# The last few microseconds of an attention and mixer kernel: order of the last chunks, and columns of the last stores

## The chip, the cores and the metric

One core of a Trainium2 chip. The metric is the device time of one execution in microseconds (us). A time is some 2 us longer than the span that the profile shows (the profiled run of the kernel before took 406.0 us and its span is 403.9 us).

## The reference, cut to what matters

```python
# batch 8, 12 heads, 448 rows, head 64; d_model 768, d_tok 256, d_ch 1536
x  = attention(normalised q, normalised k, v)          # 8 x 448 x 768
u  = x + (relu(x.T @ w_tok1) @ w_tok2).T               # mixes the rows
out = u + relu(u @ w_ch1) @ w_ch2                      # mixes the channels
```

Only the last product, `relu(...) @ w_ch2`, the addition of `u` and the store of `out` are touched by the change.

## The kernel before

The 448 rows of a batch are three chunks of 128 rows and 64 rest rows. The rest rows of two batches are done together as one chunk of 128 partitions (`m == NC`), with the odd batch. For each chunk the second channel product is done in two halves of 384 columns, each 12 matmuls into PSUM (the memory that matmuls write), and the addition of `u` on VectorE writes the half into `ost`, a tile in SBUF (the memory that stores are read from here). When both halves are there, the chunk is stored. The chunk of rest rows goes to two places in memory, so it needs two stores of 64 rows.

```python
    def m_ch2(b, m, dh):
        ...
        for ct in range(CT):                                   # CT = 12
            nc.tensor.matmul(psF[:], gt[:, ct, lo:lo + P], wc2t[:, ct, dh * DH:(dh + 1) * DH], ...)
        nc.vector.tensor_tensor(out=o[:, dh * DH:(dh + 1) * DH]..., in0=psF[:]..., in1=urt[b]..., op=ALU.add)
        if dh == NDH - 1:
            if m < NC:
                nc.sync.dma_start(out=out[b, 0:SM].rearrange("(p c) d -> c p d", c=NC)[m], in_=o[:])
            else:
                nc.sync.dma_start(out=out[b - 1, SM:S, :], in_=o[0:XR])      # XR = 64
                nc.sync.dma_start(out=out[b, SM:S, :], in_=o[XR:P])

    def ch_units(b):
        return ([...m_ch1(b, ct)... for ct in range(CT)]
                + [(ns(DH, 12), lambda m=m, dh=dh: m_ch2(b, m, dh))
                   for m in range(NC + b % 2) for dh in range(NDH)])         # rest rows last
```

Of the kernel before, what the change touches and what calls it, by code (L numbers as in the profile page):

```python
# [7 lines left out]
FP32 = mybir.dt.float32  # L8
FP16 = mybir.dt.float16
AF = mybir.ActivationFunctionType  # L10
ALU = mybir.AluOpType
# [11 lines left out]
def kernel(  # L23
# [12 lines left out]
    nc = tc.nc  # L36

    B, H, S, E = q.shape
# [4 lines left out]
    P = 128  # L43
    NC = 3
    SM = P * NC
    XR = S - SM
    E1 = E + 1
    DT = D // P
    CT = C // P
    TT = T // P  # L50
    DH = 384
    NDH = D // DH
# [17 lines left out]
    ps = ctx.enter_context(tc.tile_pool(name="ps", bufs=4, space=bass.MemoryType.PSUM))  # L70
# [8 lines left out]
    wc2t = cst.tile([P, CT, D], FP16, name="wc2t")  # L79
# [12 lines left out]
    pairt, urt = {}, {}  # L92
# [287 lines left out]
    def m_ch1(b, ct):  # L380
        ut, gt = pairt[b // 2]
        sp = slice(S * (b % 2), S * (b % 2 + 1))
        psG = ps.tile([P, S], FP32, name=f"psG_{b}_{ct}", tag="b")
        for dt in range(DT):
            nc.tensor.matmul(psG[:], wc1t[:, dt, ct * P:(ct + 1) * P], ut[:, dt, sp],  # L385
                             start=(dt == 0), stop=(dt == DT - 1))
        nc.scalar.activation(out=gt[:, ct, sp], in_=psG[:], func=AF.Relu)  # L387

    ost = {}

    def m_ch2(b, m, dh):
        gt = pairt[b // 2][1]
        lo = SM if m == NC else (512 * (b % 2) + P * m)
        if dh == 0:
            ost[0] = outp.tile([P, D], FP32, name=f"ost_{b}_{m}", tag="ost")
        o = ost[0]
        psF = ps.tile([P, DH], FP32, name=f"psF_{b}_{m}_{dh}", tag="b")
        for ct in range(CT):
            nc.tensor.matmul(psF[:], gt[:, ct, lo:lo + P], wc2t[:, ct, dh * DH:(dh + 1) * DH],  # L399
                             start=(ct == 0), stop=(ct == CT - 1))  # L400
        j = m if b % 2 == 0 else (m + 1) % 4
        nc.vector.tensor_tensor(out=o[:, dh * DH:(dh + 1) * DH].rearrange("p (i d) -> p i d", i=3),  # L402
                                in0=psF[:].rearrange("p (i d) -> p i d", i=3),
                                in1=urt[b][:, 3 * dh:3 * dh + 3, j, :], op=ALU.add)
        if dh == NDH - 1:
            if m < NC:
                nc.sync.dma_start(out=out[b, 0:SM].rearrange("(p c) d -> c p d", c=NC)[m], in_=o[:])
            else:
                nc.sync.dma_start(out=out[b - 1, SM:S, :], in_=o[0:XR])
                nc.sync.dma_start(out=out[b, SM:S, :], in_=o[XR:P])  # L410



    def ns(cols, n=1):
        return n * cols / 2.4

    def ch_units(b):
        return ([(ns(S, DT), lambda ct=ct: m_ch1(b, ct)) for ct in range(CT)]
                + [(ns(DH, 12), lambda m=m, dh=dh: m_ch2(b, m, dh))
                   for m in range(NC + b % 2) for dh in range(NDH)])  # L420

    queue = []
    fed = [0.0]
# [58 lines left out]
    with tc.manual_schedule():  # L482
# [5 lines left out]
            name=nc.get_next_instruction_name(), act_func_set_id=ACT_SET_LN_EXP,  # L488
# [34 lines left out]
        w = ps.tile([P, 512], FP32, name="busy", tag="b")  # L523
# [36 lines left out]
        for i in range(NP_ALL + 2):  # L560
# [27 lines left out]
            def tok2(p):  # L588
                m_tok2(p)
                if p % NPAIR == NPAIR - 1:  # L590
                    queue.extend(ch_units(p // NPAIR))
# [133 lines left out]
```

## Time and profile before

| | before |
|---|---|
| median of 6 runs, first comparison | 406.39 us (406.03 to 407.37) |
| span of the profiled run | 403.9 us |
| TensorE busy | 96% |
| end of the last matmul | 398.95 us |
| from there to the end of the span ("the tail") | 4.95 us |

In the views PE is TensorE, PEld its weight loads, DVE VectorE, ACT ScalarE, POOL GpSimd; SPq and ACTq are the sync and the scalar queue, from which stores are issued. A store's data move some time after its issue, as packets on 16 DMA engines; it has landed when all of it is reported done.

The head of the page of the kernel before, and its chain of waits (shares of the span):

```profile
span 403.9 us, 9103 instructions
PE 389.7 (96%) x3646; PEld 225.6 (56%) x3646; DVE 204.9 (51%) x463; ACT 226.4 (56%) x407; POOL 208.8 (52%) x306
...
PE 77%; POOL 6%; issue 5%; ACT 5%; DVE 4%; SPq 1%; DMA 1%; POOLq 0%; DVEq 0%
```

TensorE is busy nearly everywhere, so without fewer matmuls time can be won only where it has nothing to do. That is 403.9 - 389.7 = 14.2 us in all: 4.66 us in the first 20 us (the windows view shows it busy for 15.34 of them), 4.6 us scattered, and 4.95 us at the end, with which the change deals. The timeline of the kernel before, from 383 us (TensorE alone) and then from 399 us (all engines); the columns are start, duration, engine, line, operation:

```profile
383.19 15.76 PE L399 MATMUL psF<-wc2t,gt 128*128 128x384 f16 x96
```

```profile
398.99 0.56 DVE L402 TENSOR_TENSOR ost<-psF,ur 128x384 f32<-128x384 f32 x1 [1.39 <-PE psF L399]
399.58 0.50 SPq L409 DMA_DIRECT2D out_dram<-ost  x1
400.13 0.58 SPq L410 DMA_DIRECT2D out_dram<-ost  x1
```

The 96 matmuls of the last batch's four chunks end at 383.19 + 15.76 = 398.95 us. What follows is serial: an addition, two issues, the landing of their data, and the closing semaphores.

In the DMA view (from issue to landing, last number, us) the stores of the last chunk stand against it:

```profile
out_dram<-ost SPq DMA_DIRECT2D x2, 192.0 KB, 2.7
```

```profile
out_dram<-ost SPq DMA_DIRECT2D x1, 384.0 KB, 2.3
```

### The profile page before, as it was taken

The numbers are of one execution on the slowest core, as the hardware profiler recorded it, in microseconds if no ns is written. First come the engines' busy times: TensorE is split into PE (matmuls) and PEld (weight loads), VectorE is DVE, ScalarE is ACT, GpSimd is POOL, SyncE is SP. The second block draws the span as 40 slices with busy tenths as digits, with TensorE's granted clock in tenths as the row PEclk, the third lists the DMA queues.
The fourth block names the chain that finished last, engine by engine and source line by source line (L and its number), as shares of the span: only waits on it lengthen the run. The fifth ranks groups of instructions, "written<-read, shape, count | busy, mean of one in ns | idle before, by whom it ended". The sixth has DMA issues, their size and how long they took to land.

```text
span 403.9 us, 9103 instructions
## 1 busy us (share of the span) xinstructions
PE 389.7 (96%) x3646; PEld 225.6 (56%) x3646; DVE 204.9 (51%) x463; ACT 226.4 (56%) x407; POOL 208.8 (52%) x306
## 2 busy tenths in 40 slices
PE   7799999999999999999999999999999999999995
PEld 3356465565555565555555565555555565565562
DVE  5698689574444655355544654455534342242021
ACT  6998699633766356654756436664766435611400
POOL 5987495795292939385673909476773400000000
PEclk9699999999999999999999999999999999999998
DMA  8999999999792978989893798979882643023012
GB/s 223 283 270 261 219 242 199 225 231 197 184 204 52 250 177 211 182 213 179 232 202 60 227 147 214 212 149 236 185 132 50 141 97 67 15 66 93 2 78 78
DMA packets 137194, 67.51 MB, mean 167 GB/s; under 512 B 93184, under 2 KB 133568, under 8 KB 137152
## 3 DMA queue, kind: packets, MB, share of 16 engines
q1 hardware_dynamic: 132976, 61.36, 70.5%
q0 software_dynamic: 3632, 5.18, 7.2%
q8 instruction: 28, 0.46, 0.5%
q10 hardware_dynamic: 544, 0.39, 0.3%
q14 instruction: 14, 0.11, 0.1%
HBM read 43.38 MB, written 11.01 MB: 135 GB/s over the span
## 4 chain that ended last, share of the span: by engine, by line
PE 77%; POOL 6%; issue 5%; ACT 5%; DVE 4%; SPq 1%; DMA 1%; POOLq 0%; DVEq 0%
PE psF L399 24%; PE psG L385 23%; PE psO L318 7%; PE psS L297 7%; PE psR L338 4%; PE psU L357 4%; PE psX L304 3%; ACT pt L298 2%; PE psO L320 2%; POOL kq L207 2%; POOL sq L176 2%; POOL kq L218 1%; PE pst L239 1%; POOL sqx L176 1%; DVE ssq L189 1%
## 5 line engine op out<-in xcount | busy, mean ns | idle before, releaser
L298 ACT ACTIVATE pt<-psS 128x896 f16<-128x896 f32 x141 | 124.0, 915 | 71.6 <-PE psS L297 71.3
L385 PE MATMUL psG<-ut,wc1t 128*128 128x448 f16 x576 | 122.5, 353 | 0.0
L399 PE MATMUL psF<-wc2t,gt 128*128 128x384 f16 x672 | 117.1, 326 | 0.6 <-ACT pt L305 0.6
L387 ACT ACTIVATE gt<-psG 128x448 f16<-128x448 f32 x96 | 52.3, 545 | 79.2 <-PE psG L385 79.0
L207 POOL TENSOR_TENSOR kq<-km,rn 128x384 f16<-128x384 f32 x47 | 39.7, 844 | 101.9 <-ACT rn L200 93.2
L399 PEld LDWEIGHTS <-gt 128*128 128x128 f16 x672 | 63.4, 98 | 42.6 <-issue 4.7
L385 PEld LDWEIGHTS <-wc1t 128*128 128x128 f16 x576 | 52.5, 98 | 46.2 <-issue 5.2
L402 DVE TENSOR_TENSOR ost<-psF,ur 128x384 f32<-128x384 f32 x56 | 31.2, 557 | 81.0 <-PE psF L399 77.5
L318 PEld LDWEIGHTS <-pt 128*128 128x128 f16 x1152 | 52.3, 98 | 16.7 <-issue 5.6
L318 PE MATMUL psO<-vt,pt 128*128 128x65 f16 x1152 | 57.9, 194 | 0.1
L189 DVE TENSOR_REDUCE ssq<-sq 128x12 f32<-128x768 f32 (+1 forms) x49 | 45.2, 932 | 17.9 <-POOL sq L176 14.4
L297 PE MATMUL psS<-qk 64*128 64x448 f16 x282 | 44.0, 360 | 1.2 <-ACT pt L298 1.2
L324 DVE TENSOR_TENSOR x<-psO,rec 128x256 f16<-128x256 f32 x96 | 40.8, 424 | 3.3
L320 PE MATMUL psO<-vx,pt 128*128 128x130 f16 x192 | 42.0, 219 | 0.0
L207 POOL TENSOR_TENSOR kq<-qm,rn 128x384 f16<-128x384 f32 x47 | 39.0, 830 | 0.0
L323 DVE RECIPROCAL rec<-psO 128x4 f32<-128x4 f32 x96 | 17.1, 178 | 41.0 <-PE psO L320 40.8
L176 POOL TENSOR_TENSOR sq<-km 128x384 f32<-128x384 f32 x42 | 34.5, 824 | 2.5 <-DMA km<-in_k_dram 2.4
L367 DVE TENSOR_TENSOR ut<-psU,xT 128x448 f16<-128x448 f32 (+2 forms) x39 | 17.6, 477 | 26.2 <-PE psU L357 17.8
L338 PE MATMUL psR<-x,w1t 128*128 128x128 f16 x384 | 29.4, 219 | 0.1
L297 PEld LDWEIGHTS <-qk 64*128 64x128 f16 x282 | 10.5, 94 | 30.6 <-issue 27.4
L357 PE MATMUL psU<-w2t,r 128*128 128x448 f16 x96 | 25.9, 353 | 1.6 <-DVE x L324 0.8
L305 ACT ACTIVATE pt<-psX 128x448 f16<-128x448 f32 x48 | 26.1, 544 | 0.0
(75 smaller groups left out, 339.9 us busy)
## 6 DMA issues: line engine op xcount, KB each, us to landing
vm<-in_v_dram SPq DMA_DIRECT2D x16, 576.0 KB, 7.1
out_dram<-ost SPq DMA_DIRECT2D x24, 384.0 KB, 2.9
qm<-in_q_dram SPq DMA_DIRECT2D x15, 576.0 KB, 5.1
km<-in_k_dram SPq DMA_DIRECT2D x15, 576.0 KB, 6.9
wc1t<-in_moe_w_ch_dram POOLq DMA_DIRECT2D x2, 1152.0 KB, 13.3
wc2t<-in_moe_w_ch_dram POOLq DMA_DIRECT2D x2, 1152.0 KB, 13.2
out_dram<-ost SPq DMA_DIRECT2D x8, 192.0 KB, 2.8
xq<-in_q_dram SPq DMA_DIRECT2D x7, 192.0 KB, 7.8
```

The source lines that it names most:

```text
L176: eng.tensor_tensor(out=out, in0=src, in1=src, op=ALU.mult)
L189: nc.vector.tensor_reduce(out=ssqs[p // HP % 3][:, lo + 6 * a0:lo + 6 * a1], in_=sq[p][:, a0:a1].rearrange("p a g e -> p (a g) e"), axis=A ...
L207: eng.tensor_tensor(out=kqs[n % 2][:, j, a, 0:NC, :].rearrange("p c (g e) -> p g c e", g=2), in0=src, in1=_bcast_free(rn, E), op=ALU.mult)
L297: nc.tensor.matmul(psS[:, g, 0:S], qk[r, P * c:P * (c + 1)], qk[r, 512:512 + S], start=True, stop=True)
L298: nc.scalar.activation(out=pt[:, 2 * S * c:2 * S * (c + 1)].rearrange("p (g s) -> p g s", g=2), in_=psS[:, :, 0:S], func=AF.Exp, scale=inv ...
L318: nc.tensor.matmul(psO[:, mm, E1 * g:E1 * (g + 1)], pt[:, at:at + P], vt[:, 2 * j + g, c, 0:E1], start=(g == 0 and c == 0), stop=False)
L320: nc.tensor.matmul(psO[:, mm, :], pt[:, PX + lo:PX + lo + P], vx[:, j, 0:2 * E1], start=False, stop=True)
L338: nc.tensor.matmul(psR[:, tt, :], w1t[:, m, tt * P:(tt + 1) * P], xs[p][:, m, :], start=(m == 0), stop=(m == NC))
L357: nc.tensor.matmul(psU[:], rs[p][:, tt, :], w2t[:, tt, lo:lo + S], start=(tt == 0), stop=by_dma and tt == TT - 1)
L385: nc.tensor.matmul(psG[:], wc1t[:, dt, ct * P:(ct + 1) * P], ut[:, dt, sp], start=(dt == 0), stop=(dt == DT - 1))
L387: nc.scalar.activation(out=gt[:, ct, sp], in_=psG[:], func=AF.Relu)
L399: nc.tensor.matmul(psF[:], gt[:, ct, lo:lo + P], wc2t[:, ct, dh * DH:(dh + 1) * DH], start=(ct == 0), stop=(ct == CT - 1))
```

## The change

Its intent is to shorten the serial tail: the rest rows with their two stores go two chunks earlier, and the last chunk's second half is done as 256 and then 128 columns. Each of its parts is stored by itself, so that only 64 KB are left to store after the last matmul.

```diff
-    def m_ch2(b, m, dh):
+    def m_ch2(b, m, i0, i1, send=False):        # columns 128*i0 to 128*i1
...
-        if dh == NDH - 1:
+        if send or i1 == DT:
+            cols = slice(P * ost[1], P * i1)     # what is not stored yet
+            ost[1] = i1
             if m < NC:
-                nc.sync.dma_start(out=...[m], in_=o[:])
+                nc.sync.dma_start(out=...[m][:, cols], in_=o[:, cols])
             else:
-                nc.sync.dma_start(out=out[b - 1, SM:S, :], in_=o[0:XR])
-                nc.sync.dma_start(out=out[b, SM:S, :], in_=o[XR:P])
+                nc.sync.dma_start(out=out[b - 1, SM:S, cols], in_=o[0:XR, cols])
+                nc.sync.dma_start(out=out[b, SM:S, cols], in_=o[XR:P, cols])
...
+        last = b == B - 1
+        for m in (0, NC, 1, 2) if last else range(NC + b % 2):
+            for i0, i1 in ((0, 3), (3, 5), (5, 6)) if last and m == 2 else ((0, 3), (3, 6)):
+                units.append((ns(P * (i1 - i0), CT), lambda m=m, i0=i0, i1=i1:
+                              m_ch2(b, m, i0, i1, last and m == 2)))
```

More of the change, by code (lines that the diff above doesn't have):

```diff
@@ L389 @@
     ost = {}
-    def m_ch2(b, m, dh):
+    def m_ch2(b, m, i0, i1, send=False):
         gt = pairt[b // 2][1]
         lo = SM if m == NC else (512 * (b % 2) + P * m)
-        if dh == 0:
+        if i0 == 0:
             ost[0] = outp.tile([P, D], FP32, name=f"ost_{b}_{m}", tag="ost")
-        o = ost[0]
-        psF = ps.tile([P, DH], FP32, name=f"psF_{b}_{m}_{dh}", tag="b")
+            ost[1] = 0
+        o, w = ost[0], P * (i1 - i0)
+        psF = ps.tile([P, DH], FP32, name=f"psF_{b}_{m}_{i0}", tag="b")
         for ct in range(CT):
-            nc.tensor.matmul(psF[:], gt[:, ct, lo:lo + P], wc2t[:, ct, dh * DH:(dh + 1) * DH],
+            nc.tensor.matmul(psF[:, 0:w], gt[:, ct, lo:lo + P], wc2t[:, ct, P * i0:P * i1],
                              start=(ct == 0), stop=(ct == CT - 1))
         j = m if b % 2 == 0 else (m + 1) % 4
-        nc.vector.tensor_tensor(out=o[:, dh * DH:(dh + 1) * DH].rearrange("p (i d) -> p i d", i=3),
-                                in0=psF[:].rearrange("p (i d) -> p i d", i=3),
-                                in1=urt[b][:, 3 * dh:3 * dh + 3, j, :], op=ALU.add)
-        if dh == NDH - 1:
+        nc.vector.tensor_tensor(out=o[:, P * i0:P * i1].rearrange("p (i d) -> p i d", d=P),
+                                in0=psF[:, 0:w].rearrange("p (i d) -> p i d", d=P),
+                                in1=urt[b][:, i0:i1, j, :], op=ALU.add)
+        if send or i1 == DT:
+            cols = slice(P * ost[1], P * i1)
+            ost[1] = i1
             if m < NC:
-                nc.sync.dma_start(out=out[b, 0:SM].rearrange("(p c) d -> c p d", c=NC)[m], in_=o[:])
+                nc.sync.dma_start(out=out[b, 0:SM].rearrange("(p c) d -> c p d", c=NC)[m][:, cols], in_=o[:, cols])
             else:
-                nc.sync.dma_start(out=out[b - 1, SM:S, :], in_=o[0:XR])
-                nc.sync.dma_start(out=out[b, SM:S, :], in_=o[XR:P])
+                nc.sync.dma_start(out=out[b - 1, SM:S, cols], in_=o[0:XR, cols])
+                nc.sync.dma_start(out=out[b, SM:S, cols], in_=o[XR:P, cols])
     def ns(cols, n=1):
@@ L417, in ch_units @@
     def ch_units(b):
-        return ([(ns(S, DT), lambda ct=ct: m_ch1(b, ct)) for ct in range(CT)]
-                + [(ns(DH, 12), lambda m=m, dh=dh: m_ch2(b, m, dh))
-                   for m in range(NC + b % 2) for dh in range(NDH)])
+        units = [(ns(S, DT), lambda ct=ct: m_ch1(b, ct)) for ct in range(CT)]
+        last = b == B - 1
[3 more added lines that the diff above has]
+                              m_ch2(b, m, i0, i1, last and m == 2)))
+        return units
     queue = []
```

## The prediction

> **What bounds the kernel now.** The page shows TensorE busy for 389.7 of 403.9 us (96%) at a granted clock of 0.989, and the chain of waits is 77% PE. The change leaves all of that alone except the last few microseconds. In the timeline the last chunk-mix matmuls (psF, L399) run without a gap from 383.19 to 398.95 us, so from there back PE is the bound; after 398.95 the span is a serial tail of 4.95 us in which no matmul runs:
> - the last addition ost<-psF, 384 columns: 398.99 to 399.55 (558 ns);
> - two stores of rest rows, 64 rows of 3072 B each, issued one after the other on the sync queue: 399.58 for 0.50 us, 400.13 for 0.58 us;
> - their data moves from about 400.7 to 402.4 (windows of half a microsecond: DMA share 0.65, 1.02, 0.87, 0.56, then 0), landing about 2.7 us after the issue, i.e. near 403.0;
> - about 0.9 us of closing drains and semaphores.
>
> **What the change does.**
> 1. *Moves* the rest rows two chunks earlier. Their double store then hides under about 8 us of matmuls. Their buffer is reused by the last chunk only 5.9 us later, while the stores need some 3.5 us, so I expect no wait.
> 2. The last store becomes one issue. A 128-row store of 3072 B rows now takes 0.33 us to issue and lands in 2.3 us (timeline, issue at 395.7): about 0.8 us to the first packet, 1.1 us of packets (8 per engine of about 121 ns, plus spread), 0.4 us to landing. With rows of 512 B the packets shrink: the trace has 18 ns for 256 B and 36 ns for 768 B, so about 30 ns each is my estimate, and 0.4 us in all with spread. Estimated landing 1.6 to 1.9 us after the issue. The Trainium skill ("DMA: Bandwidth & Descriptors", Anatomy of one DMA) gives a fixed cost of about 2.0 us plus bytes; this trace has the 384 KB store land in 2.3 us in all, so its fixed part is nearer 1.2 us, which I use, leaning a little long.
> 3. The last addition shrinks from 384 to 128 columns: additions from PSUM take 224 ns at 64 columns and 547 at 384 (groups by form), so about 295 ns: 0.26 us off.
> 4. *Adds* 12 matmuls, 12 weight loads, one addition and two stores. Eight 128-column matmuls occupy 0.45 us of the chain (56 ns each), twelve of 384 columns 1.95 us. So 256 + 128 columns take about 1.31 + 0.67 = 1.98 us against 1.95: 0.03 us more. The extra addition is hidden; the 256-column store (128 KB) is issued about 0.5 us before the last and may delay its packets a little.
>
> **Sum on the critical path.** Serial from the end of the addition to the end of the span: now 4.35 us; afterwards 0.03 + about 1.75 + 0.9 = 2.7 us, so 1.65 off. Plus 0.26 for the addition, minus 0.04 for PE: about 1.85 us off the span. All of it is on the critical path, but it is 0.45% of the time.
>
> **Prediction:** 404.7 us, 80% range 403.9 to 405.7. Faster by over 2%: 0.01; within 2%: 0.98; slower: 0.01.
>
> **What would show it.** Right: psF matmuls gapless to about 399.0; last addition near 0.3 us; one last store with landing below 2.0 us; PE-free tail about 3.1 us instead of 4.95; no DVE wait on out_dram<-ost. Wrong step: a last store landing at 2.3 us or more (fixed latency, or queued behind the 128 KB store), matmuls of 128 columns further apart than 56 ns, or an addition that waits for an earlier part's store of the same tile (tracking per tile), which would give 1 to 2 us back.

## More of the kernel before

The windows view tells when the data moved (last three numbers of a line: granted clock, busy share of the DMA engines, GB/s):

```profile
400.60:401.00 0.40, 0.00 (x0) 0.00 (x0) 0.00 (x0) 0.00 (x0) 0.00 (x0) 1.00 0.81 184
401.00:401.40 0.40, 0.00 (x0) 0.00 (x0) 0.00 (x0) 0.00 (x0) 0.00 (x0) 1.00 0.92 184
401.40:401.80 0.40, 0.00 (x0) 0.00 (x0) 0.00 (x0) 0.00 (x0) 0.00 (x0) 0.76 0.89 238
401.80:402.20 0.40, 0.00 (x0) 0.00 (x0) 0.00 (x0) 0.00 (x0) 0.00 (x0) 0.50 1.14 346
402.20:402.60 0.40, 0.00 (x0) 0.00 (x0) 0.00 (x0) 0.00 (x0) 0.00 (x0) 0.50 0.12 31
```

The engines are busy from the start, yet they move only 184 GB/s at first. The store of a whole chunk of 128 rows, four microseconds earlier, moved up to 392 GB/s:

```profile
396.80:397.20 0.40, 0.40 (x5) 0.23 (x3) 0.16 (x1) 0.00 (x0) 0.00 (x0) 1.00 0.98 392
```

Half the bytes took longer to land than the whole.

## The result, and the profile after

| | before | after |
|---|---|---|
| median of 6 runs | 406.39 us (406.03 to 407.37) | 404.70 us (403.98 to 406.61) |
| ratio, 95% interval | | 0.996 (0.9936 to 0.9984) |
| span of the profiled run | 403.9 us | 403.5 us |
| last matmul ends | 398.95 us | 400.66 us |
| tail | 4.95 us | 2.87 us |

A ratio is the mean time of one kernel's runs over that of the other's of the same rounds, so not quite the ratio of the medians. The interval excludes 1. Later, with 5 more rounds on one chip, the same kernel had 0.9946 (0.9919 to 0.9973).

The page's head and chain after the change, the matmuls of the last batch in the timeline, and the timeline from 400.9 us:

```profile
span 403.5 us, 9133 instructions
PE 388.2 (96%) x3658; PEld 225.8 (56%) x3658; DVE 204.9 (51%) x464; ACT 226.6 (56%) x407; POOL 209.3 (52%) x306
...
PE 74%; POOL 8%; ACT 5%; DVE 4%; DMA 4%; issue 3%; SPq 1%; ACTq 0%; POOLq 0%; DVEq 0%
```

```profile
384.86 15.79 PE L400 MATMUL psF<-wc2t,gt 128*128 128x384 f16 x108
```

```profile
400.69 0.29 DVE L403 TENSOR_TENSOR ost<-psF,ur 128x128 f32<-128x128 f32 x1 [0.24 <-PE psF L400]
401.01 0.33 SPq L410 DMA_DIRECT2D out_dram<-ost  x1
```

The chunk matmuls take 15.79 us instead of 15.76, with 12 more of them. The addition fell from 0.56 to 0.29 us, one issue of 0.33 us replaced two of 0.50 and 0.58, and the DMA view of the end (396 to 404 us) shows landing times that fall with size:

```profile
out_dram<-ost SPq DMA_DIRECT2D x1, 384.0 KB, 2.3
out_dram<-ost SPq DMA_DIRECT2D x1, 192.0 KB, 1.9
out_dram<-ost SPq DMA_DIRECT2D x1, 128.0 KB, 1.7
out_dram<-ost SPq DMA_DIRECT2D x1, 64.0 KB, 1.5
```

(The 192 KB here are half the columns of 128 rows. The 192 KB of 64 rows before took 2.7 us.)

So the tail is 2.08 us shorter. But the two spans differ by only 0.38 us, because the last matmul ended 1.70 us later. Whoever compares only this pair of profiles reads either "0.4 us" or "the change made the matmuls late". The timed runs say 1.7 us. Where the 1.70 us arose is to be seen in the windows of the two traces (first number after the window: its length, then TensorE busy). Before, then after:

```profile
80.00:100.00 20.00, 19.43 (x203) 12.55 (x202) 11.67 (x26) 7.47 (x13) 14.30 (x20) 1.00 1.07 214
260.00:280.00 20.00, 20.00 (x201) 11.60 (x200) 11.72 (x29) 11.12 (x20) 14.30 (x20) 1.00 0.91 186
```

```profile
80.00:100.00 20.00, 18.71 (x189) 11.78 (x188) 12.21 (x25) 7.61 (x13) 16.57 (x23) 1.00 1.17 236
260.00:280.00 20.00, 19.38 (x198) 11.51 (x197) 11.24 (x28) 11.13 (x19) 13.74 (x20) 1.00 0.95 198
```

TensorE lost 0.72 and 0.62 us there, 1.34 of the 1.70, over a hundred microseconds before the first changed instruction (the instructions up to the last batch's second chunk stand in the same order in both). Matched one by one, the matmuls after fall behind by 1.03 us between 80 and 100 us and by 0.60 us between 260 and 280. In the first 40 us TensorE was busy for 1.84 us less after than before, but by 40 us the matmuls were level to 0.03 us. The theory must therefore say whether this is chance.

### The profile page after: what moved, and what is told of

Read it like the earlier page. It is cut to its first block, busy times and chain, and to the rows that moved or that the text cites. A ratio compares the mean times of both kernels' runs of the same rounds, so it can differ in the third digit from the quotient of the medians.

```text
span 403.5 us, 9133 instructions
## 1 busy us (share of the span) xinstructions
PE 388.2 (96%) x3658; PEld 225.8 (56%) x3658; DVE 204.9 (51%) x464; ACT 226.6 (56%) x407; POOL 209.3 (52%) x306
## 4 chain that ended last, share of the span: by engine, by line
PE 74%; POOL 8%; ACT 5%; DVE 4%; DMA 4%; issue 3%; SPq 1%; ACTq 0%; POOLq 0%; DVEq 0%
PE psF L400 24%; PE psG L385 23%; PE psO L318 7%; PE psS L297 6%; PE psR L338 4%; PE psU L357 4%; PE psX L304 2%; DMA km<-in_k_dram 2%; ACT pt L298 2%; POOL kq L207 2%; PE psO L320 2%; POOL sq L176 2%; POOL kq L218 2%; POOL sqx L176 1%; DVE ssq L193 1%
## 5 line engine op out<-in xcount | busy, mean ns | idle before, releaser
L400 PE MATMUL psF<-wc2t,gt 128*128 128x384 f16 (+2 forms) x684 | 117.2, 323 | 1.3 <-DVE ost L403 0.7
L403 DVE TENSOR_TENSOR ost<-psF,ur 128x384 f32<-128x384 f32 (+2 forms) x57 | 31.3, 550 | 79.1 <-PE psF L400 77.8
```

The source lines that it names most:

```text
L400: nc.tensor.matmul(psF[:, 0:w], gt[:, ct, lo:lo + P], wc2t[:, ct, P * i0:P * i1], start=(ct == 0), stop=(ct == CT - 1))
```

## The experiments

**Theory A.** The gain is the shorter serial tail and nothing else; its terms are the order (no double store of 64 rows at the end), the smaller addition and the smaller last store. What precedes the tail jitters from run to run, whatever the kernel. **Rival B.** The change itself also made earlier stages later, and took part of the gain back. **Rivals within the tail:** only the small store counts; or what made the old end slow was the second issue, and not the 64-row stores as such.

Twelve kernels ran, all with correct results. The tail is the span less the end of the last matmul (its modelled end, as for all matmuls). Each has one profile, and 6 timed runs beside 11 of the kernel before on its own chip. The first job is a1 and e1 to e3, the second e4 to e7, the third b1 and e8 to e10.

| run | last matmul ends, us | tail, us | median, us | ratio to before (95%) |
|---|---|---|---|---|
| before (first profile) | 398.95 | 4.95 | 406.39 | |
| b1_before_again | 399.03 | 4.96 | 406.91 | 1.0001 (0.9986 to 1.0017) |
| e6_two_queues | 398.96 | 4.99 | 406.56 | 0.9996 (0.9976 to 1.0016) |
| e2_split_only | 401.10 | 4.98 | 406.63 | 0.9997 (0.9975 to 1.0020) |
| e8_upper_first | 398.92 | 4.86 | 406.60 | 1.0004 (0.9987 to 1.0021) |
| e7_row_halves | 398.90 | 4.83 | 406.45 | 0.9991 (0.9972 to 1.0010) |
| e1_order_only | 398.84 | 4.05 | 405.46 | 0.9973 (0.9951 to 0.9995) |
| e3_one_store | 399.05 | 3.77 | 405.03 | 0.9961 (0.9936 to 0.9985) |
| e4_halves_stored | 402.12 | 3.52 | 405.25 | 0.9971 (0.9945 to 0.9998) |
| e10_640_then_128 | 400.41 | 3.25 | 404.97 | 0.9956 (0.9940 to 0.9972) |
| e5_two_of_64 | 399.76 | 3.10 | 404.48 | 0.9948 (0.9923 to 0.9972) |
| a1_again (the change) | 402.20 | 2.88 | 404.19 | 0.9946 (0.9919 to 0.9973) |
| e9_64_two_queues | 398.91 | 2.77 | 404.42 | 0.9939 (0.9923 to 0.9955) |

The intervals are 0.3 to 0.5% wide, 1.3 to 2.2 us, so they separate the upper group (tail near 4.9) from the lowest row, but not neighbours. In every row the gain in the tail (4.95 us less the row's tail) lies within the interval of its timed ratio. The tails are the finer measure: two profiles of one kernel agree within 0.01 us (4.95 and 4.96, 2.87 and 2.88).

### a1: the change again (no edit)

> The changed kernel again, unaltered. Theory A (the gain is the serial tail alone, and everything before the last chunk only jitters from run to run): the tail from the end of the last matmul to the end of the span is again 2.8 to 2.9 us, against 4.95 before, while the time of the last matmul's end differs from the 400.7 us of the first profile by up to 2 us either way. Rival B (the change itself made the stages before the tail later, 400.7 against 399.0 us): the last matmul ends again near 400.7 us or later. Ratio to before 0.995 to 0.997.

The tail was 2.88 us and the last matmul ended at 402.20 us, later still: within the 2 us of theory A, but as rival B has it too, so this run decides only about the tail. The ratio, 0.9946, is just under the 0.995 to 0.997 expected. Its six times went from 403.67 to 406.85 us and the spans from 401.9 to 405.1. The profiled run was the slowest of the six. Some 2.7 of the 3.2 us by which its matmuls lay behind those of the kernel before arose in the first 20 us, where its chain of waits (start, duration) held

```profile
11.85 7.32 DMA xk<-in_k_dram
19.25 0.36 ACT sqx L174
19.61 0.81 ACT pt L298
```

a load of 7.3 us that is not among the listed pieces of the same stretch in the second profile of the kernel before.

### b1: the kernel before again (no edit)

> The kernel before, unaltered, for a second profile. Theory A (the stages before the tail jitter whatever the kernel): the tail is again 4.95 us within 0.05 us, while the last matmul may end anywhere from 398.8 to 402.2 us, the range the variants showed. Ratio 1.000 within 0.002. Rival B (only changed kernels start the tail late): not supported if it ends later than 399.5 us; one run near 399.0 us would leave it as it is.

The tail was 4.96 us and the last matmul ended at 399.03 us, so this profile by itself leaves rival B open. It falls on the others: e1, e3 and e9 contain the new order, e3 and e9 also the smaller parts, and their last matmuls ended at 398.84, 399.05 and 398.91 us, within 0.2 us of the two profiles of the kernel before. And the kernel before jitters as well: in the first job its eleven times went from 405.90 to 408.92 us and its spans from 403.8 to 406.8. The fastest runs of the two kernels in that job differ by 405.90 - 403.67 = 2.2 us, about what the tails differ by. Take the tail of a kernel as fixed, as the two pairs of profiles suggest; then the span of each timed run less this tail is an estimate of when its last matmul ended. The median is 399.75 us for 39 runs of the kernel before (398.8 to 401.9), 399.8 for the 12 runs of the change (399.0 to 402.2) and 399.7 for all 60 runs with the new order. So the late matmuls of single profiles are jitter that both kernels have; what B could still hide is a few tenths of a microsecond.

### e1: order only

```diff
-            for i0, i1 in ((0, 3), (3, 5), (5, 6)) if last and m == 2 else ((0, 3), (3, 6)):
+            for i0, i1 in ((0, 3), (3, 6)):
-                              m_ch2(b, m, i0, i1, last and m == 2)))
+                              m_ch2(b, m, i0, i1)))
```

> The rest rows go two chunks earlier, but the last chunk keeps two halves of 384 columns and one store of 384 KB. If the terms add up as I think, the tail is 0.03 + 0.56 + 0.03 + 2.3 to landing + about 0.95 of closing = 3.9 us, 1.05 us less than before: half of the gain comes from the order alone. Rival (the gain is all in the small last store): tail near 4.9 us.

The tail was 4.05 us (3.9 expected). Moving the rest rows alone takes 0.90 us off. The rival fell. The end of its timeline:

```profile
398.88 0.56 DVE L403 TENSOR_TENSOR ost<-psF,ur 128x384 f32<-128x384 f32 x1 [1.39 <-PE psF L400]
399.46 0.34 SPq L410 DMA_DIRECT2D out_dram<-ost  x1
```

### e2: split only, rest rows still last

```diff
-        for m in (0, NC, 1, 2) if last else range(NC + b % 2):
-            for i0, i1 in ((0, 3), (3, 5), (5, 6)) if last and m == 2 else ((0, 3), (3, 6)):
+        for m in range(NC + b % 2):
+            for i0, i1 in ((0, 3), (3, 5), (5, 6)) if last and m == NC else ((0, 3), (3, 6)):
```

(and `m == NC` in the last argument as well)

> The rest rows stay last, but their second half is done as 256 and 128 columns, each part stored by itself, which for the rest rows means two stores of 64 rows per part. Theory: the sync queue issues two stores per part (0.50 + 0.58 us), so the stores of the 256 columns are still being issued when the last addition is done; tail 3.6 us without that backlog, about 4.2 us with it. So the two halves of the change are not independent. Rival (independent terms): tail near 4.95 minus 0.9 us, with no issue wait.

The tail was 4.98 us, no shorter than without the split: a miss, by 0.8 us, in the direction of the theory. The timeline:

```profile
400.97 0.55 SPq L412 DMA_DIRECT2D out_dram<-ost  x1
401.14 0.29 DVE L403 TENSOR_TENSOR ost<-psF,ur 128x128 f32<-128x128 f32 x1 [0.24 <-PE psF L400]
401.58 0.59 SPq L413 DMA_DIRECT2D out_dram<-ost  x1
402.26 0.55 SPq L412 DMA_DIRECT2D out_dram<-ost  x1
402.86 0.59 SPq L413 DMA_DIRECT2D out_dram<-ost  x1
```

The last addition was done at 401.43 us, but the last store was issued at 402.86: three parts of two stores each queue up on the sync queue, one start every 0.6 to 0.7 us. So the two halves of the change are not independent. The split alone gives nothing (+0.03 us), the order alone 0.90, both together 2.08.

### e3: new order, small parts, one store at the end

```diff
-                              m_ch2(b, m, i0, i1, last and m == 2)))
+                              m_ch2(b, m, i0, i1)))
```

> The new order and the columns computed as 384, 256 and 128, but one store of all 384 KB at the end. Expected tail 0.03 + 0.29 + 0.03 + 2.3 + 0.95 = 3.6 us: against order only it shows the smaller addition alone (0.27 us), and against the full change the smaller last store alone (0.75 us).

The tail was 3.77 us (3.6 expected). From e1 to e3 only the computation is split: 0.28 us, which is the smaller addition (0.56 to 0.29 us). From e3 to the full change only the store is split: 0.90 us (0.75 expected).

### e4: new order, two halves, each stored by itself

```diff
-            for i0, i1 in ((0, 3), (3, 5), (5, 6)) if last and m == 2 else ((0, 3), (3, 6)):
+            for i0, i1 in ((0, 3), (3, 6)):
```

> The new order, the last chunk as two halves of 384 columns, each stored by itself (192 KB, rows of 1536 B). A store of this size landed in 1.9 us in the profile after. Expected tail 0.03 + 0.56 + 0.03 + 1.9 + 0.95 = 3.5 us. With order only (3.9 expected) and the full change (2.85 measured) this gives tail against size of the last store.

The tail was 3.52 us, as expected. With the addition as in e1, halving the last store from 384 to 192 KB gave 0.53 us.

### e5: the last 128 columns as 64 and 64

```diff
-            for i0, i1 in ((0, 3), (3, 5), (5, 6)) if last and m == 2 else ((0, 3), (3, 6)):
+            for i0, i1 in ((0, 3), (3, 5), (5, 5.5), (5.5, 6)) if last and m == 2 else ((0, 3), (3, 6)):
```

(on the changed kernel, as are e1 to e4 and e10; with the slices and the addition written for 64 columns)

> As the full change, but the last 128 columns are done and stored as 64 and 64, with rows of 256 B in the last two stores. By the read packets of this trace (18 ns for 256 B, 27 ns for 512 B) and the additions from PSUM (224 ns at 64 columns) the tail falls by 0.1 to 0.15 us to about 2.7 us. Rival (stores of rows under 512 B cost extra because each is a read and a write, as the Trainium skill says in DMA: Bandwidth & Descriptors, Specifications): the packets of 256 B take more than 50 ns and the tail is no shorter than 2.85 us.

The tail was 3.10 us, longer than with 128 columns, but not for the rival's reason: the packets of 256 B took 18 ns each by the packet records of the trace, against 27 ns for 512 B. The timeline:

```profile
399.80 0.22 DVE L405 TENSOR_TENSOR ost<-psF,ur 128x64 f32<-128x64 f32 x1
```

```profile
400.45 0.40 SPq L415 DMA_DIRECT2D out_dram<-ost  x1
```

The addition ended at 400.02 us and its store was issued 0.43 us later, because the sync queue was busy with the two stores before it (starts at 399.55, 399.98 and 400.45 us). I had left this out of the expectation, though e2 was built on it.

### e9: the same, with the store before the last on the scalar queue

```diff
-                nc.sync.dma_start(out=...[m][:, cols], in_=o[:, cols])
+                (nc.scalar if i1 == 5.5 else nc.sync).dma_start(out=...[m][:, cols], in_=o[:, cols])
```

(on e5)

> As the 64 and 64 run, but the store before the last is issued from the scalar queue. There the last store was issued 0.42 us after its addition was done, since the sync queue had issued two stores just before. If the sync queue's issuing is the limit: last issue right after the addition, tail 2.70 us, 0.17 us better than the change. If the stores share one generator of descriptors whichever queue issues them (as the two-queue run suggests): the issue comes early, but the landing does not, and the tail stays at 2.95 us or more.

The tail was 2.77 us (2.70 expected, 2.95 or more by the rival). In the timeline the scalar queue's store starts between the two of the sync queue:

```profile
398.70 0.83 SPq L415 DMA_DIRECT2D out_dram<-ost  x2
398.85 0.37 ACTq L415 DMA_DIRECT2D out_dram<-ost  x1
```

So in e5 it was the issuing. This version's tail beats the change's by 0.10 us; its time (0.9939 against 0.9946 and 0.996) cannot be told from it.

### e6: the kernel before, the second rest store on the scalar queue

```diff
-                nc.sync.dma_start(out=out[b, SM:S, :], in_=o[XR:P])
+                (nc.scalar if b == B - 1 else nc.sync).dma_start(out=out[b, SM:S, :], in_=o[XR:P])
```

> The kernel before, with the second of the last two rest stores issued from the scalar queue instead of the sync queue, so that both are issued at once. If the second issue (0.55 us later) is what its landing waits for: tail 4.4 us, and the packets of both run side by side near 122 ns. Rival (the data itself is the limit, 192 packets' worth of slow rows at about 213 ns): the data still ends about 1.7 us after its first packet and the tail stays within 0.15 us of 4.95.

The tail was 4.99 us: the expectation fell and its rival held. Both stores were issued at the same moment, and it did not help. Timeline, and the landing from the DMA view:

```profile
399.58 0.50 SPq L409 DMA_DIRECT2D out_dram<-ost  x1
399.58 0.54 ACTq L410 DMA_DIRECT2D out_dram<-ost  x1
```

```profile
out_dram<-ost SPq DMA_DIRECT2D x1, 192.0 KB, 2.7
out_dram<-ost ACTq DMA_DIRECT2D x1, 192.0 KB, 3.2
```

By the packet records the sync queue's 64 packets started between 400.73 and 401.69 us, with a mean of 251 ns, and the scalar queue's between 401.74 and 402.33, with a mean of 123 ns. The second store's data began only when the first's had all started, although both had been issued together. So the old end was not slow for its second issue.

### e7 and e8: a chunk stored as two halves of its rows

```diff
-                nc.sync.dma_start(out=...[m][:, cols], in_=o[:, cols])
+                for r in (slice(0, XR), slice(XR, P)) if b == B - 1 and m == 2 else (slice(0, P),):
+                    nc.sync.dma_start(out=...[m][r, cols], in_=o[r, cols])
```

(on e1; e8 has the two slices in the other order)

> The new order with two halves of 384 columns, and the last chunk's store cut into two stores of 64 rows each, one after the other on the sync queue, rows and places in memory as in the order-only kernel. If stores of 64 partitions are slow in themselves (packets about 213 ns against 122, first packet 1.15 us after the issue against 0.8): tail 4.9 us, as before the change. Rival (only rest rows, which lie in one piece in memory, are slow): packets 122 ns, tail 4.2 to 4.4 us.

> As the row-halves run, but the upper 64 rows (partitions 64 to 127) are stored first. In that run the first store's packets took 209 to 257 ns and the second's about 121 ns. If being first of two stores of 64 rows is what makes them slow: the same picture, tail 4.8 us. If partitions 0 to 63 are slow in themselves: now the second store is the slow one, and its packets over 200 ns come last; tail about 5 us.

The tails were 4.83 and 4.86 us, 0.78 and 0.81 more than with the same chunk stored at once (e1: 4.05). The DMA view of the end of e7, then of e1 (GB/s in 40 slices of about 0.13 us):

```profile
GB/s 0 0 0 0 0 0 0 0 0 0 0 0 0 169 217 265 120 265 145 241 121 338 386 386 313 96 24 0 0 0 0 0 0 0 0 0 0 0 0 0
out_dram<-ost SPq DMA_DIRECT2D x2, 192.0 KB, 2.6
```

```profile
GB/s 0 0 0 0 0 0 0 0 0 0 0 189 402 402 425 378 378 402 378 71 0 0 0 0 0 0 0 0 0 0 0 0 0 0 0 0 0 0 0 0
out_dram<-ost SPq DMA_DIRECT2D x1, 384.0 KB, 2.3
```

By the packet records (64 packets of 3072 B to a store), the first 64 to start averaged 231 ns in e7 and 232 in e8, the next 32 averaged 124 in both, and the last 32 178 and 183, whether partitions 0 to 63 or 64 to 127 went first. (The "about 121 ns" in the expectation of e8 holds only for the first half of the second store.) So it is neither the place of the rest rows in memory nor the half of SBUF: a chunk stored as two stores of 64 rows, one behind the other, is slow, and its first store is the slower one. Why the first store of such a pair runs its packets at half speed was not settled; no run has a store of 64 rows alone, so whether it takes a pair is open too.

### e10: 640 columns, then 128

```diff
-                              m_ch2(b, m, i0, i1, last and m == 2)))
+                              m_ch2(b, m, i0, i1, last and m == 2 and i1 == 5)))
```

> The changed kernel, computed as 384, 256 and 128 columns, but stored as 640 columns and then 128: one store less, yet 320 KB instead of 128 KB just ahead of the last one. If the last store's packets queue behind those of the store before it: 320 KB take about 0.95 us of packets, the last landing comes 0.3 us later, tail about 3.2 us. If they interleave or the small store passes: tail stays at 2.87 us, and storing the first 384 columns early is worth nothing.

The tail was 3.25 us (3.2 expected). The DMA view from 400 us shows the last store, of the same 64 KB, landing 0.4 us later after its issue than in the change:

```profile
out_dram<-ost SPq DMA_DIRECT2D x1, 320.0 KB, 2.2
out_dram<-ost SPq DMA_DIRECT2D x1, 64.0 KB, 1.9
```

Its packets start at 401.90 us, as those of the store before it run out (the last of these began at 401.95). Storing the first 384 columns early is what clears the way: 0.38 us.

## Why the prediction was right

The time, 404.7 us, was met, and the mechanism held; some of that exactness is luck, since the median of six runs of a kernel that varies by 3 us is not known to 0.1 us. Two errors also met there: the tail gained 2.08 us and not 1.85, while the two medians differ by only 1.69.

- **"After 398.95 the span is a serial tail of 4.95 us."** Right. Every variant's gain is found in the tail: the order 0.90, the smaller addition 0.28, the smaller last store 0.90, together 2.08 us (e1, e3, full change, each on top of the one before). The prediction had 1.85.
- **The smaller addition, 0.26 us, and 0.03 us more of matmuls.** 0.27 us (558 to 291 ns), and 15.79 against 15.76 us.
- **"Estimated landing 1.6 to 1.9 us ... I use, leaning a little long" (about 1.75).** This is the term that was mis-sized: 1.5 us by the page of the first profile, 1.6 by that of the second. The packets of 512 B took 27 ns (estimated 30). The fixed part of 1.2 us read from the 384 KB store was right and the leaning was not. It explains most of the 0.23 us by which the tail, 2.87 us, came out shorter than the 3.1 predicted.
- **The 128 KB store "may delay its packets a little".** Not seen: the last store's first packet came 0.85 us after its issue, against 0.83 for a store with none ahead of it. With 320 KB ahead it was delayed (e10).
- **No wait of the addition for an earlier part's store.** Right; no addition waited for one in the last 20 us.
- **"psF matmuls gapless to about 399.0."** Gapless, yes, but they ended at 400.66 us. As a check this line was badly made: it took a moment that jitters by some 3 us between executions for a fixed one. Tail and last matmul's end have to be read apart.
- **What the prediction did not see:** it listed the old end's second issue (0.55 us later) as one of its costs, and e6 shows that removing it wins nothing; the two 64-row stores run one behind the other however they are issued.

## What to carry to other kernels

When an engine is busy to the end, look at what is serial after its last instruction: put a chunk that needs two stores, or stores of fewer partitions, well before the last, and leave little to add and store at the end. Splitting the last store pays only while the issuing queue is free when the last part is ready and the part before it is small enough to be out of the way (e2, e5 and e10 show both limits). When the gain is below the jitter of an execution, measure the segment that the change touches in each profile and let timed rounds confirm the sign.

## What the Trainium skill lacked or had wrong

- "DMA: Bandwidth & Descriptors", Rules for kernel authors: it says that two transfers to disjoint partition halves serialize because they share the engines, and that packets from two queues interleave. The first half agrees (tails of 4.83 and 4.86 us against 4.05 in one store). The second did not show in e6: from two queues, the second store's first packet started at 401.74 us, after the last of the first at 401.69. In e9 packets of both queues were under way together (from 400.05 to 400.20 us), so when they mix is open. "SBUF — State Buffer", Door 1, gives a transfer of 64 partitions a lower rate than one of 128; that fits the first store of e6 (177 to 184 GB/s) and not the second (392 GB/s at its best). That the two of a pair differ so stands on no page.
- "DMA: Bandwidth & Descriptors", Anatomy of one DMA: about 2.0 us fixed plus bytes over 436 GB/s. The page gives this fit for the gpsimd path; the prediction had set it beside stores of the sync queue without saying so. An estimate from it would be 2.15 us for 64 KB and 2.9 for 384 KB; here they landed in 1.5 to 1.6 and in 2.3 us. A fit for the sync and scalar path is missing there.
- "DMA: Bandwidth & Descriptors", Issuing engines are not separate DMA queues: issuing from several engines "will only save the time on the sequencer it takes to initiate the DMA, which is usually small relative to the DMA itself". In a serial tail it was not small: 3.10 us with one queue, 2.77 with two (e5, e9), with the starts of waiting stores on the sync queue 0.43 to 0.68 us apart (e5 and e2) beside landings of 1.5 to 2.2 us.
- "DMA: Bandwidth & Descriptors", Specifications: below 512 B a read-modify-write. Stores of 256 B rows took 18 ns a packet and those of 512 B 27 ns, so per byte a third more, but no step that a tail of a microsecond would notice.
- "Perfetto Trace Analysis", DMA Optimizations: splitting may let the whole finish sooner where engines are idle. It agrees (3.77 to 2.87 us, e3 to the change), but the item gives no figure for the time on the issuing queue, which was the limit here (e2: 4.98 us).
